# A Fourier, MLP and routing kernel: routing units, weight conversion and the hand-over to the kept tokens moved

## The chip, the cores and the metric

The kernel runs on one core of a Trainium2 chip. The metric is the time on the device, in microseconds (us), of one execution. Of the kernel before there are three timed runs, with a median of 1934.6 us, and one profiled execution.

A core has five engines that run their own queues in order: TensorE (PE, matmuls and transposes), VectorE (DVE), ScalarE (ACT), GpSimd (POOL) and SyncE (SP, which here only issues DMAs). They meet through semaphores. PSUM is the memory that PE writes to, SBUF the one that all of them read.

## The reference

```python
def _attn_ref(x):                        # x: 8 x 3072 x 256
    X = np.fft.fft(x, axis=1)
    X = np.fft.fft(X, axis=2)
    return X.real.astype(np.float32)

def _moe_ref(x, w_in, w_out, alpha):     # 256 -> 2048 -> 256
    h = x @ w_in
    g = np.maximum(h, 0.0) + alpha * np.minimum(h, 0.0)
    return (g @ w_out).astype(np.float32)

def _moe2_ref(x, w_gate, w1, w2, capacity):   # 8 experts, capacity 768
    logits = x @ w_gate
    expert_idx = np.argmax(logits, axis=1)
    probs = softmax(logits)                   # written out in the reference
    gate_w = probs[np.arange(N), expert_idx]
    ...                  # tokens in order: the first 768 of each expert are kept
    h = np.maximum(np.einsum('ecd,edf->ecf', disp, w1), 0.0)
    y = np.einsum('ecf,efd->ecd', h, w2)
    ...                  # out[i] = gate_w[i] * y[expert, pos] if kept, else 0
```

The 8 batches are flattened to 24576 tokens before the MLP. Each expert keeps 768, so at most 6144 tokens need the MLP in full; the others need only their gate logits, and an output row of zeros.

## The kernel before

**Three stretches.** The first 59.5 us load constants and weights and do stage 1 of the Fourier transform of batch 0. Then come eight batches, to 1068 us, which compute gate logits of all tokens and route them. From 1091.9 us to the end 16 tiles of 384 kept tokens (8 experts, two tiles each) go through the MLP and their expert.

**A batch** has 32 steps, numbered (b, s), each a call of `fstep`: six matmuls q, a copy qs of q by ACT (L494), qm by DVE (L495), six matmuls p, and mp and mm by DVE (L505, L506). q has one PSUM buffer and p two. Every fourth step (s % 4 == 1; in batch 0 every step) a logit block follows: 4 calls of `logit`, 32 matmuls that reduce mp and mm to gate logits.

**What else runs in a step** stands in three lists filled by `at(list, b, t, fn, ...)`, where t counts steps from the start of batch b: `pre` runs ahead of `fstep`, `early` between qm and the p matmuls, `late` behind the logit block (L837 to 846). Since every engine's queue is in order, this sets what stands behind what. In these lists are, for the batches to come: the load of x (SP), its fold (xf, POOL or DVE), fsplit (fh on ACT, fl on POOL), stage 1 (matmuls into an mi buffer of PSUM, then the copy zw on ACT, L255), stage 2 (s), transp, and split.

**In batch 0** the weights are converted as well. `conv_a` and `conv_b` take a chunk i of w_in (k = "i") or w_out (k = "o") apart: an ACT Square into a tile m (L366), then DVE; `conv_c` finishes on POOL. m has two buffers, which wf of `w_cs` shares (L395). `w_cs`, `w_t`, `w_b` and `w_h` turn chunks into the tables of the logits, on PE, ACT and DVE. Chunk i is used at steps around s = 4 i.

**The route units of a batch** run inside the next one. `ltrans` turns logits (ls) by three transposes and copies them back (lst, ACT). u0: maximum and dd on DVE, exp on ACT (L575). u1: one-hot of the expert (DVE). u2: matmuls that count tokens ahead of each in its expert, into mi, the copy pc (ACT, L595), the addition of the counts so far (carry), and the sum of the exps. u3: the slot number idx of each token (DVE). Then 24 scatters (`us`): POOL copies one column of the latest mm to `gate` (L627), which ties the scatter to that step, and issues an indirect DMA of 128 records (L628).

**The hand-over** (L847 on): `ltrans` and the route units of the last batch without steps around them, then `rows`, which finds the table rows of the first 9 x 128 slots by a product of one-hot matrices (hotp, from DVE; hotr, from DVE and POOL) instead of reading back a scatter. Then POOL gathers three times 128 rows (L942), DVE turns signs (L953), PE transposes, and the first tile starts. In a tile, step f of `hstep` makes h (PE), ng (ACT, L978), g (DVE, L979), gh (ACT, L980) and gl (POOL, in the first tile DVE, L981); `ystep` uses gh and gl three steps later. W1 and W2 of the first expert are split in two parts by `split_w` (ACT copy and DVE subtraction, L934 and L935). `heat` issues matmuls whose result is not used.

## Time and profile before

| | |
|---|---|
| timed runs, median of 3 | 1934.6 us (1932.71 to 1936.72) |
| the profiled execution's own time | 1926.48 us |
| its span | 1924.7 us |
| mean granted clock of TensorE, share of full speed | 0.986 |
| PE busy | 1865.5 us, 97% |
| DVE busy | 1191.6 us, 62% |
| ACT busy | 851.0 us, 44% |
| POOL busy | 1109.7 us, 58% |

All rows are of the profiled execution; its start is 0. PE is busy for nearly all of the span, so the other engines matter where PE waits for them. A row of an instruction names its engine, line, operation and what it writes and reads (out<-in), with buffer numbers left out. What stands in brackets at its end is how long the engine had been idle, and what it waited for last.

### The profile page before, as it was taken

What the parts mean: (1) busy time and instruction counts of PE and PEld (TensorE: products, weight loads), DVE (VectorE), ACT (ScalarE), POOL (GpSimd) and SP (SyncE); (2) the same over time, 40 slices, a digit from 0 to 9 for tenths busy, and PEclk for the clock granted to TensorE, in tenths of its full rate; (3) what the DMA queues carried; (4) which work ended last, traced back from release to release, by engine and by line L of the source; (5) the groups of instructions that cost most, each with busy time, mean ns of one, the idle gap of its engine ahead of it and who ended that gap; (6) DMA issues with size and microseconds to landing.
All of it is one profiled execution on the core that took longest, in us unless ns stands there. A gap on an engine that the chain in (4) does not pass through costs nothing. (4 is left out here: it accounts for less than half of the span.)

```text
span 1924.7 us, 33959 instructions
## 1 busy us (share of the span) xinstructions
PE 1865.5 (97%) x12965; PEld 1604.0 (83%) x12965; DVE 1191.6 (62%) x1684; ACT 851.0 (44%) x1712; POOL 1109.7 (58%) x1230
## 2 busy tenths in 40 slices
PE   8899999999999999999999899999999999999997
PEld 5676687777777777777777699999999999999997
DVE  4799588878989989898899653333333333333331
ACT  3445455444344343443322254545444444444452
POOL 3675394867767676674435375645455555555452
PEclk9799999999999999999999999999999999999999
DMA  9644345444353443433310301101111111101000
GB/s 262 203 147 133 103 156 189 128 131 149 105 165 118 142 153 109 161 116 113 101 34 1 141 16 62 34 33 36 37 39 39 39 36 39 40 15 61 15 9 17
DMA packets 126259, 174.48 MB, mean 91 GB/s; under 512 B 20060, under 2 KB 80285, under 8 KB 125488
## 3 DMA queue, kind: packets, MB, share of 16 engines
q1 hardware_dynamic: 115056, 157.99, 25.8%
q0 software_dynamic: 10752, 12.23, 2.3%
q8 instruction: 102, 1.67, 0.4%
q10 hardware_dynamic: 288, 2.10, 0.3%
q14 instruction: 61, 0.50, 0.1%
HBM read 94.71 MB, written 78.40 MB: 90 GB/s over the span
## 5 line engine op out<-in xcount | busy, mean ns | idle before, releaser
L981 POOL TENSOR_TENSOR gl<-g,gh 128x384 fp32r<-128x384 f32 x240 | 243.4, 1014 | 324.1 <-ACT gh L980 323.1
L495 DVE SCALAR_TENSOR_TENSOR qm<-er,w,qs 128x780 f32<-128x780 f32 x256 | 322.6, 1260 | 119.1 <-ACT qs L494 115.8
L494 ACT COPY qs<-q 128x780 f32<-128x780 f32 x256 | 207.6, 811 | 335.7 <-PE q L491 159.3
L979 DVE SCALAR_TENSOR_TENSOR g<-ng,om,h 128x384 f32<-128x384 f32 x256 | 157.1, 614 | 313.8 <-ACT ng L978 272.4
L993 PE MATMUL y<-gh,WO 128*128 128x384 f32 x1024 | 262.2, 337 | 0.0
L505 DVE SCALAR_TENSOR_TENSOR mp<-p,qs 128x780 f32<-128x780 f32 x256 | 245.7, 960 | 5.2 <-PE p L501 5.2
L506 DVE TENSOR_TENSOR mm<-p,qm 128x780 f32<-128x780 f32 x256 | 244.8, 956 | 0.0
L628 POOL DMA_INDIRECT rec<-recs,idx x192 | 197.3, 1028 | 56.0 <-issue 45.7
L980 ACT CAST gh<-g 128x384 fp32r<-128x384 f32 x256 | 131.6, 514 | 197.9 <-DVE g L979 197.9
L978 ACT ACTIVATE ng<-h 128x384 f32<-128x384 f32 x256 | 125.8, 491 | 176.4 <-PE h L972 176.2
L518 PE MATMUL lg<-mp,Vn 128*32 128x384 f32 x1024 | 187.7, 493 | 0.2 <-DVE mp L505 0.2
L993 PEld LDWEIGHTS y<-gh,WO 128*128 128x128 f32 x1024 | 186.8, 188 | 0.0
L518 PE MATMUL lg<-mm,Vp 128*32 128x384 f32 x1024 | 184.3, 493 | 0.1
L993 PE MATMUL y<-gl,WO 128*128 128x384 f32 x512 | 172.7, 337 | 0.0
L1015 DVE SCALAR_TENSOR_TENSOR z<-z,z 128x384 fp32r<-128x384 f32 x128 | 71.3, 557 | 162.2 <-ACT z L1014 162.2
L627 POOL COPY gate<-mm 128x1 f32<-128x1 f32 x168 | 79.0, 470 | 137.9 <-DVE mm L506 137.8
L1025 PE MATMUL o<-W,z 128*128 128x256 f32 x1152 | 154.7, 284 | 1.2 <-ACT ot L1028 1.2
L1025 PEld LDWEIGHTS o<-W,z 128*128 128x128 f32 x1152 | 146.9, 190 | 1.6 <-ACT ot L1028 1.6
L238 POOL TENSOR_TENSOR fl<-xf,fh 128x512 fp32r<-128x512 f32 x72 | 96.5, 1341 | 79.3 <-ACT fh L237 68.2
L1012 PE MATMUL z<-yh,W 128*128 128x384 f32 x512 | 130.5, 335 | 0.4
L518 PEld LDWEIGHTS lg<-mp,Vn 128*32 128x32 f32 x1024 | 55.6, 110 | 88.2 <-issue 84.2
L501 PE MATMUL p<-Ah,w20r 128*128 128x390 f32 x256 | 92.3, 361 | 5.2 <-DVE mm L506 5.1
(353 smaller groups left out, 4537.6 us busy)
## 6 DMA issues: line engine op xcount, KB each, us to landing
x<-x SPq DMA_DIRECT2D x96, 256.0 KB, 3.4
zd<-zw SPq DMA_DIRECT2D x96, 256.0 KB, 2.1
out_dram<-zero SPq DMA_DIRECT2D x64, 384.0 KB, 4.6
zk<-zd SPq DMA_DIRECT2D x240, 96.0 KB, 2.8
r<-w SPq DMA_DIRECT2D x16, 1024.0 KB, 5.6
abtab<-tm SPq DMA_DIRECT2D x60, 256.0 KB, 2.4
er<-erd SPq DMA_DIRECT2D x16, 390.0 KB, 4.4
rawi<-w_in SPq DMA_DIRECT2D x8, 512.0 KB, 4.4
```

Source lines behind the costliest of these rows:

```text
L494: A.copy(qs, q[:, :, 0:SB])
L495: V.scalar_tensor_tensor(out=qm, in0=e, scalar=w2[:, f : f + 1], in1=qs, op0=ALU.mult, op1=ALU.add)
L505: V.scalar_tensor_tensor(out=mp, in0=p[:, :, 0:SB], scalar=-1.0, in1=qs, op0=ALU.mult, op1=ALU.min)
L506: V.tensor_tensor(out=mm, in0=p[:, :, 0:SB], in1=qm, op=ALU.max)
L518: PE.matmul(l[32 * gi : 32 * gi + 32, 0:384], lhsT=w, rhs=v, start=start, stop=stop)
L628: d = G.indirect_dma_start(out=rec, out_offset=bass.IndirectOffsetOnAxis(ap=st["idx"][:, i : i + 1], axis=0), in_=recs[:, b].rearrange("p ...
L979: V.scalar_tensor_tensor(out=g, in0=ng, scalar=om[:, f : f + 1], in1=ps, op0=ALU.mult, op1=ALU.add)
L980: A.copy(gh, g)
L981: (V if i == 0 else G).tensor_tensor(out=gl, in0=g, in1=gh.bitcast(F32), op=ALU.subtract)
L993: PE.matmul(d["yp"][m][:, 0:384], lhsT=w[:, f, ms], rhs=x, start=(f == 0 and n == 0), stop=(f == NF - 1 and n == 2))
L1012: PE.matmul(ps, lhsT=w[:, kd, ms], rhs=x, start=(n == 0), stop=(n == 5))
L1025: PE.matmul(ps, lhsT=x[:, m, js], rhs=w[:, m, :], start=(m == 0 and n == 0), stop=(m == 7 and n == 2))
```

## The change

Five edits, in the words of what they do:

1. The conversion of chunk 3 of w_in and w_out (`conv_a`, `conv_b`, `conv_c`, and the load of the next chunk) runs one step later in batch 0. The loads of x of the second batch, from its third block, run one step later.
2. All route units run in `late`, and u2 is cut in two: u2 keeps the matmuls and the copy pc, u2b has the addition of the counts, the update of carry and the sum of the exps (`norm`).
3. The steps of these units and of the scatters change: for the units of the second to sixth batch the scatters stand at steps 18 to 41, so that the last ten run in the batch after. The last ones stand at steps 10 to 30, three steps having two.
4. In the hand-over the last batch reads PSUM without the copies lst and pc, leaves carry as it is, and runs `norm` behind the gathers. Of the one-hot matrix hotp DVE makes 16 of 24 columns, and ACT the others as Relu(1 - (iota - p)^2), from a new tile npj = -p. The product takes four columns of DVE and two of ACT in turn.
5. The W1 split of the first expert moves from ahead of the signs into steps f = 8 to 11 of the first tile. The transposes of the first tile run gather by gather, with 5 heat matmuls between.

The names in the excerpts below carry the batch and the step or chunk: mi3 is m of chunk 3 of w_in, zw1_2 is zw of batch 1, block 2, qs3_0_5 is qs of batch 3, half 0, step 5. Several rows of an instruction with the same operands are one row with a count.

ACT in batch 0, steps 1 and 2, first before and then after:

```order
L366 ACTIVATE mo2_904<-rawo2_783 128x512
L366 ACTIVATE mi3_916<-rawi3_849 128x512
L255 COPY zw1_2_924<-mi_921 128x512
L494 COPY qs0_1_1_943<-q0_1_1_936 128x780
L437 COPY uu1_954<-mi_947 64x256
L441 COPY wgs_116<-mi_947 128x2x8
```

```order
L367 ACTIVATE mo2_903<-rawo2_782 128x512
L256 COPY zw1_2_917<-mi_914 128x512
L495 COPY qs0_1_1_936<-q0_1_1_929 128x780
L438 COPY uu1_947<-mi_940 64x256
L442 COPY wgs_117<-mi_940 128x2x8
L397 COPY wf2_963<-mi_958 128x512
L400 CAST w10r_954<-wf2_963 128x256
L400 CAST w12r_956<-wf2_963 128x256
L402 ACTIVATE wr2_967<-wf2_963 1x2x128
L367 ACTIVATE mi3_988<-rawi3_848 128x512
L256 COPY zw1_3_996<-mi_993 128x512
```

The Square mi3 stood ahead of zw1_2; it now stands nine rows later, directly ahead of zw1_3.

ACT in batch 3, steps 2 to 6, where the route units of batch 2 run (lst2, ex2, pc2), first before and then after:

```order
L494 COPY qs3_0_2_5800<-q3_0_2_5793 128x780
L237 CAST fh4_10_5815<-xf4_10_5728 128x512
L553 COPY lst2_5824<-mi_5820 128x384
L477 CAST Bh3_1_5836<-Bf3_4729 128x780
L494 COPY qs3_0_3_5853<-q3_0_3_5846 128x780
L575 ACTIVATE ex2_5861<-dd2_5859 128x192
L494 COPY qs3_0_4_5881<-q3_0_4_5874 128x780
L255 COPY zw4_10_5892<-mi_5885 128x512
```

```order
L495 COPY qs3_0_4_5841<-q3_0_4_5834 128x780
L256 COPY zw4_10_5852<-mi_5845 128x512
L238 CAST fh4_11_5866<-xf4_11_5798 128x512
L555 COPY lst2_5875<-mi_5871 128x384
L478 CAST Ah3_1_5885<-Af3_4671 128x780
L495 COPY qs3_0_5_5907<-q3_0_5_5900 128x780
L578 ACTIVATE ex2_5943<-dd2_5941 128x192
L495 COPY qs3_0_6_5964<-q3_0_6_5957 128x780
```

The exp stood between the qs copies of steps 3 and 4; it now stands between those of steps 5 and 6.

DVE in the hand-over, from the counts of the last batch to the row numbers, first before and then after:

```order
L598 TENSOR_TENSOR tp7_12662<-pc7_12660,carry_81 128x192
L599 TENSOR_TENSOR carry_81<-pc7_12660,carry_81 128x8
L602 TENSOR_REDUCE sm7_12665<-ex7_12635 128x24
L603 TENSOR_SCALAR sm7_12665<-sm7_12665 128x24
L604 RECIPROCAL recs_80<-sm7_12665 128x24
L608 TENSOR_TENSOR tp7_12662<-tp7_12662,oh_84 128x192
```

```order
L606 TENSOR_TENSOR tp7_12659<-mi_12642,carry_81 128x192
L620 TENSOR_TENSOR tp7_12659<-tp7_12659,oh_85 128x192
L622 TENSOR_REDUCE pos7_12662<-tp7_12659 128x24
L624 TENSOR_SCALAR ov7_12664<-pos7_12662 128x24
L625 SCALAR_TENSOR_TENSOR pos7_12662<-r7_12638,pos7_12662 128x24
```

The four rows between the two tp rows are gone from here; three of them (L614 to L616) now stand behind the row numbers, and the product with oh follows at once.

The diff, cut:

```diff
@@
+    npj = cp.tile([128, 24], F32, name="npj")
@@
             PE.transpose(ps[:, j, :], ls[:, 128 * j : 128 * j + 128], ident)
-        lt2 = sp.tile([128, 384], F32, name=f"lst{b}", tag="ls", bufs=1)
-        A.copy(lt2.rearrange("p (j r) -> p j r", j=3), ps)
-        v0 = lt2.rearrange("p (j g a e) -> p g a j e", j=3, g=4, e=8)
+        if b < NB - 1:
+            lt2 = sp.tile([128, 384], F32, name=f"lst{b}", tag="ls", bufs=1)
+            A.copy(lt2.rearrange("p (j r) -> p j r", j=3), ps)
+            ps = lt2.rearrange("p (j r) -> p j r", j=3)
+        v0 = ps.rearrange("p j (g a e) -> p g a j e", g=4, e=8)
         for pi in range(2):
@@
                 PE.matmul(ps[:, :, q + 1 :, :], lhsT=rk[:, 4, :], rhs=ohs[:, q : q + 1, :].unsqueeze(1).to_broadcast([128, 2, 12 - q, 8]), start=False, stop=(q == 11), skip_group_check=True)
-            pc = rt([128, 2, 13, 8], "pc")
-            A.copy(pc, ps)
-            ps = pc
+            if b < NB - 1:
+                pc = rt([128, 2, 13, 8], "pc")
+                A.copy(pc, ps)
+                ps = pc
+            st["ps"] = ps
+
+        def u2b():
+            ps = st["ps"]
             t = rt([128, 2, 12, 8], "tp")
             V.tensor_tensor(out=t, in0=ps[:, :, 0:12, :], in1=carry.unsqueeze(1).unsqueeze(1).to_broadcast([128, 2, 12, 8]), op=ALU.add)
-            V.tensor_tensor(out=carry, in0=ps[:, 0, 12, :], in1=carry, op=ALU.add)
             st["t"] = t
+            if b < NB - 1:
+                V.tensor_tensor(out=carry, in0=ps[:, 0, 12, :], in1=carry, op=ALU.add)
+                norm()
+
+        def norm():
             sm = rt([128, 24], "sm")
@@
                 V.tensor_copy(pjf, pj)
+                V.tensor_scalar(out=npj, in0=pj[:, 0], scalar1=-1.0, scalar2=None, op0=ALU.mult)
             V.scalar_tensor_tensor(out=idx, in0=pj[:, 0], scalar=float(NJ), in1=pj[:, 1], op0=ALU.mult, op1=ALU.add)
@@
-        return [u0, u1, u2, u3], [us(i) for i in range(24)]
+        return [u0, u1, u2, u2b, u3], [us(i) for i in range(24)], norm
@@
         if i > 1:
-            for k, t in (("i", s - 10), ("o", s - 8)) if i > 2 else (("i", 1), ("o", 2)):
+            for k, t in (("i", s - 10 + (i == 3)), ("o", s - 8 + (i == 3))) if i > 2 else (("i", 1), ("o", 2)):
                 at(late, 0, t, conv_a, k, i)
@@
                 if c > 1:
-                    at(pre, 0, c - 3, load_x, nb, c)
+                    at(pre, 0, c - 2, load_x, nb, c)
                     at(pre, 0, c - 1, fold, nb, c)
@@
         if nb < NB:
-            rl, r1 = ((13, 14, 15, 17, 18), 19) if nb == 1 else ((6, 7, 8, 9, 10), 11) if nb == 2 else ((2, 3, 4, 5, 6), 7)
+            if nb == 1:
+                rl, r1 = (14, 15, 17, 19, 21, 23), range(24, 48)
+            elif nb < NB - 1:
+                rl, r1 = (4, 5, 9, 11, 13, 17), range(18, 42)
+            else:
+                rl, r1 = (2, 3, 5, 6, 7, 9), sorted([*range(10, 31), 13, 17, 21])
             at(late, nb, rl[0], ltrans, b)
-            ru, rs = route_units(b)
-            for i in range(4):
-                at(late if i == 2 else early, nb, rl[i + 1], ru[i])
+            ru, rs, _ = route_units(b)
+            for i in range(5):
+                at(late, nb, rl[i + 1], ru[i])
             for i in range(24):
-                at(pre, nb, r1 + i, rs[i])
+                at(pre, nb, r1[i], rs[i])
 
@@
     ltrans(NB - 1)
-    ru, scat = route_units(NB - 1)
+    ru, scat, norm = route_units(NB - 1)
     HT = (13, 45, 30)
@@
 
+    one = kp.tile([128, 1], F32, name="one")
+    G.memset(one, 1.0)
+
     def rows():
@@
             G.tensor_tensor(out=R[:, w], in0=H, in1=rk[:, 6, 24 * w : 24 * w + 24].unsqueeze(2).to_broadcast([128, 24, NJ0]), op=ALU.mult)
-        for c in range(0, 24, 6):
-            hot(V, P, 0, c, c + 6)
-        for c in range(24):
+        for c in range(0, 16, 4):
+            hot(V, P, 0, c, c + 4)
+        for c in range(16, 24):
+            sq = k2.tile([128, 128], F32, name=f"sq{c}", tag="ng")
+            A.activation(out=sq, in_=iota, func=AF.Square, bias=npj[:, c : c + 1])
+            A.activation(out=P[:, c], in_=sq, func=AF.Relu, scale=-1.0, bias=one)
+        order = [4 * (k // 6) + k % 6 if k % 6 < 4 else 16 + 2 * (k // 6) + k % 6 - 4 for k in range(24)]
+        for c in order:
             PE.matmul(ps, lhsT=P[:, c], rhs=R[:, :, c], start=(c == 0), stop=(c == 23))
@@
             PE.transpose(ps[:, 128 * j : 128 * j + 128], d["gr"][:, j, 128 * w : 128 * w + 128], ident)
+        prep_x(i, w, ps)
+
+    def prep_x(i, w, ps):
+        d = tiles[i]
         h = k2.tile([128, 384], F32R, name=f"xh{i}_{w}", tag=f"xh{w}")
@@
         prep_gather(0, j)
-    for o in range(4):
-        split_w(1, o, V)
+    norm()
+    tr = [ps1.tile([128, 512], F32, name=f"tp0_{w}", tag=t) for w, t in ((0, "tp"), (1, "o"))]
+    hz = ps2.tile([128, 512], F32, name="heat", tag="z")
     for j in range(3):
         prep_sign(0, j)
-    prep_tr(0, 0)
-    prep_tr(0, 1, "o")
+        for w in range(2):
+            PE.transpose(tr[w][:, 128 * j : 128 * j + 128], tiles[0]["gr"][:, j, 128 * w : 128 * w + 128], ident)
+        if j < 2:
+            heat(hz, 5)
+    for w in range(2):
+        prep_x(0, w, tr[w])
     load_wo(A, 1)
@@
                 scat[16 * i + f]()
-            if i == 0 and f >= 12:
-                split_w(2, f - 12, V)
+            if i == 0 and f >= 8:
+                split_w(1 + f // 12, f % 4, V)
             if (i, f) == (1, 9):
```

## Rows read from the trace of the kernel before

**Rows 1.** Page, its head: the span and the number of instructions.

```profile
span 1924.7 us, 33959 instructions
```

**Rows 2.** PE's waits by releaser: us in all, number, longest in us.

```profile
PE p L501 <- DVE mm L506: 5.3, 10, 1.0
...
PE mi L431 <- ACT zw L255: 5.1, 1, 5.1
PE mi L250 <- POOL fl L238: 4.9, 4, 1.9
PE q L491 <- ACT qs L494: 4.8, 6, 1.2
```

**Rows 3.** Windows: length; PE, PEld, DVE, ACT, POOL busy (x); clock; DMA; GB/s.

```profile
82.50:92.70 10.20, 9.11 (x34) 6.67 (x34) 6.89 (x10) 3.23 (x8) 6.87 (x10) 0.50 0.58 182
...
413.60:417.00 3.40, 3.40 (x25) 2.49 (x24) 2.46 (x3) 1.19 (x3) 2.84 (x3) 0.52 0.26 88
...
1092.90:1096.30 3.40, 3.40 (x13) 3.40 (x12) 1.18 (x3) 1.34 (x3) 0.00 (x0) 0.52 0.89 352
```

**Rows 4.** Timeline of ACT, batch 0: start, length, instruction.

```profile
81.82 0.67 ACT L366 ACTIVATE mi<-rawi 128x512 f32<-128x512 f32 x1 [4.40 <-DMA rawi<-w_in]
82.39 0.57 ACT L255 COPY zw<-mi 128x512 f32<-128x512 f32 x1
...
94.28 0.59 ACT L255 COPY zw<-mi 128x512 f32<-128x512 f32 x1 [2.32 <-PE mi L250]
```

**Rows 5.** Timeline of POOL and DVE, batch 0.

```profile
85.89 1.59 POOL L384 TENSOR_TENSOR wo<-fro,mo 128x512 f32<-128x512 f32 x1
...
91.36 0.42 DVE L404 TENSOR_TENSOR w11r<-wf,w10r 128x256 fp32r<-128x256 f32 x1 [3.05 <-ACT w10r L399]
```

**Rows 6.** Timeline of PE, batches 2 and 3.

```profile
413.47 1.11 PE L305 MATMUL s<-zk,GT 48*32 48x256 f32 x16 [1.41 <-issue]
...
490.27 0.39 PE L250 MATMUL mi<-fl,fr 128*128 128x258 f32 x1 [0.95 <-POOL fl L238]
```

**Rows 7.** Page, costliest groups: busy, mean ns, idle before.

```profile
L505 DVE SCALAR_TENSOR_TENSOR mp<-p,qs 128x780 f32<-128x780 f32 x256 | 245.7, 960 | 5.2 <-PE p L501 5.2
```

**Rows 8.** Timeline of ACT, hand-over.

```profile
1069.43 0.48 ACT L553 COPY lst<-mi 128x384 f32<-128x384 f32 x1 [0.69 <-PE mi L551]
...
1073.71 0.33 ACT L595 COPY pc<-mi 128x208 f32<-128x208 f32 x1 [1.83 <-PE mi L593]
```

**Rows 9.** Timeline of DVE, hand-over.

```profile
1074.47 0.17 DVE L599 TENSOR_TENSOR carry<-pc,carry 128x8 f32<-128x8 f32 x1
...
1075.37 0.29 DVE L608 TENSOR_TENSOR tp<-tp,oh 128x192 f32<-128x192 f32 x1
...
1077.92 4.26 DVE L898 TENSOR_TENSOR hotp<-rk,pjf 128x768 bf16<-128x768 bf16 x4
...
1083.56 2.50 DVE L935 TENSOR_TENSOR W<-r,W 128x512 fp32r<-128x512 f32 x4
```

**Rows 10.** Timeline of POOL, hand-over.

```profile
1083.65 1.57 POOL L942 DMA_INDIRECT gr<-abtab,ixr  x1 [3.15 <-DVE sg L886]
...
1087.24 1.00 POOL L942 DMA_INDIRECT gr<-abtab,ixr  x1 [0.31 <-issue]
```

**Rows 11.** Timeline of ACT, batch 0, a chain of copies.

```profile
90.31 0.58 ACT L396 COPY wf<-mi 128x512 f32<-128x512 f32 x1 [3.94 <-POOL Vp L442]
90.92 0.40 ACT L399 CAST w10r<-wf 128x256 fp32r<-128x256 f32 x1
91.23 0.40 ACT L399 CAST w12r<-wf 128x256 fp32r<-128x256 f32 x1
```

**Rows 12.** Timeline of DVE, first tile.

```profile
1115.86 0.61 DVE L979 SCALAR_TENSOR_TENSOR g<-ng,om,h 128x384 f32<-128x384 f32 x1
...
1117.96 0.61 DVE L979 SCALAR_TENSOR_TENSOR g<-ng,om,h 128x384 f32<-128x384 f32 x1
...
1120.48 0.61 DVE L979 SCALAR_TENSOR_TENSOR g<-ng,om,h 128x384 f32<-128x384 f32 x1
```

## The prediction, made before the changed kernel had run

> **What bounds the kernel now.** I read the page's head first: the span of the profiled execution is 1924.7 us [rows 1], its own time 1926.48 us, and the three timed runs have a median of 1934.6 us. The difference of 8 us lies between executions, so I add up changes against the profiled execution and carry the sum over to the median. PE is the engine that the table of the profile shows as busy almost throughout, so the end moves only where PE waits, or where it runs at the lower of its two clock levels. Hence the second view, PE's waits by releaser [rows 2]. Four of its lines touch the change: p matmuls that wait for DVE's mm (5.3 us in 10 waits), the small gate product on mi that waits for ACT's zw copy (one wait of 5.1), stage 1 that waits for POOL's fl (4.9 in 4), and q matmuls that wait for ACT's qs (4.8 in 6). Third, the stretches with a low granted clock [rows 3]: 82.5 to 92.7 at 0.50, 413.6 to 417.0 at 0.52, and 1092.9 to 1096.3 at 0.52, where 1.0 is 2.4 GHz. In each of them PE comes out of a wait. A stall here costs its own length and then about as much again at half speed. Last I read the timeline of each place where these waits lie, and of the hand-over from the last batch to the first tile of kept tokens.
>
> **Batch 0: the Square of chunk 3 of w_in.** Before, ACT's queue has that Square at 81.82 us; it waits 4.40 for its DMA, and zw of stage-1 block 2 stands behind it at 82.39 although its input is long there [rows 4]. PE's 5.1 us wait is that. The first order excerpt shows the Square moved behind four later copies. What is late next: the Square shares the m buffer with the product wo on POOL, which ends at 85.89 + 1.59 = 87.48 [rows 5], so Square and the next zw (chunk 3) come at about 88.1, against 94.28 now [rows 4], which is 6.2 earlier. DVE has little slack behind that: the largest idle time of this stretch is the 3.05 us before w11r at 91.36 [rows 5], a wait for ACT, not for work. So the gain can fade; bounds 0 and -6.2, and I take **-5.5**, near the upper end, because the wait is PE's own and the half-clock stretch begins with it. The load of x a step later makes two DMAs later, with a fold three steps ahead of use; SP has nothing else waiting there. I price it at nothing (up to 1 us if a fold becomes late).
>
> **Route units behind the logit blocks, batches 1 to 7.** The units are the same DVE, ACT and PE instructions; they move. Before, u0, u1 and u3 stand between qm and the p matmuls, so mm of the step comes late and PE waits for it: 5.3 us [rows 2]. Behind a logit block PE has its 32 matmuls in hand. I leave 0.8 us for the places where the spacing is narrow: **-4.5** (bounds 0 and -5.3). In batch 2 the same backlog shows as a wait of 1.41 before the s matmuls [rows 6] and then 3.4 us at 0.52 [rows 3], which is 3.4 x 0.48 = 1.6 lost: **-3.0**.
>
> The exp on ACT waits for DVE's dd, and qs stands behind it. The second order excerpt shows ex2 before between qs of steps 3 and 4, now behind qs of step 5, which follows a logit block. The largest q wait is 1.2, in batch 7; the other five make 4.8 - 1.2 = 3.6, of which I take **-3.4**. In batch 7 u0 is late in step 3, which has no logit block; dd now stands behind mp and mm, each 0.96 us [rows 7], so the exp delays qs by up to 1.9 more: **+1.9** (bounds 0 and +1.9).
>
> Two new costs. The scatters now run from step 18 to 41 of 32, that is across the border of two batches, where POOL has xf and fl of the next-but-one x. A wait of stage 1 for fl there was 0.95 in batch 3 [rows 6]; I take three such, for batches 4 to 6: **+2.9** (bounds 0 and what the slow rival gives). u2 takes an mi buffer in a step where transp also uses one, so its matmuls wait for one ACT copy; the nearest row is 0.31 from start to start of two 128x256 casts [rows 11], in six batches: **+1.9** (bounds 0 and 4).
>
> **The hand-over.** Off the chain from the last logit block to the gathers go the lst copy (0.48, with its hand-over 0.54), the pc copy (0.33) and, between 1074.47 and 1075.37, carry and norm: 0.90 [rows 8, 9]. npj adds 0.10. Together -1.7. The one-hot P of 4.26 us [rows 9] is cut: DVE makes 16 of 24 columns, 4.26 x 16/24 = 2.84, and would begin at 1077.92 - 1.7 = 1076.2 and end at 1079.1. ACT makes the other 8 by a Square and a Relu each. No such pair stands in the trace. The nearest rows are two casts 128x256 [rows 11]: a dependent instruction starts 0.03 after the end of the one before (wf 90.31 + 0.58, w10r 90.92), an independent one 0.09 before it. For half the elements I estimate 0.29, a pair 0.29 + 0.03 + 0.29 - 0.09 = 0.52, eight 4.2 us; begun with npj, about 0.4 ahead of DVE's P, that ends at 1080.0, against 1082.18 for the old P. Bounds of a pair 0.34 (half of the pair of casts, overlapped) and 0.76 (two casts of the larger size): ends 1078.5 and 1081.9. So the end of the rows product moves by **-2.2** (bounds -3.1 and -0.3).
>
> The Trainium skill, "ScalarE: Activation LUTs", section Rules for kernel authors, budgets about 0.3 us per ACTIVATE with a bias read from a column, plus 0.83 ns an element. By it 16 of them are 16 x 0.41 = 6.5 us, ACT would end at about 1082.3, the gain of 2.2 would be gone and the time 2.2 longer; the trace has 0.40 for a cast of 256 elements without such a bias, where the rule makes 0.51, and no row with one. That lies inside the forecast's own range below.
>
> The gathers: with the W1 split beside them on DVE (1083.56, 2.50 long) the first took 1.57 us, the third without it 1.00 [rows 9, 10]. Without the split I take **-1.0** for the three (bounds 0 and -1.0). The Trainium skill, "SBUF - State Buffer", section Who interferes with whom, speaks against this: a tensor_tensor takes only the read side of the pair that DVE and GpSimd share, and descriptor generation needs the write side (it calls that inferred). By it the split never slowed the gathers and this term is 0, so the time is 1.0 longer; the rows lean the other way, but the first gather may be long as the first.
>
> The first h matmuls run at 0.52 for 3.4 us [rows 3], 1.6 lost. Now transposes and heat matmuls stand between the gathers, so I take half: **-0.8**. The W1 split goes into the first tile at f = 8 to 11. There DVE's g comes every 2.10 us without W (1115.86 to 1117.96) and 2.52 with W and a sign [rows 12]; two steps with a sign make 2 x 0.42, the two others I put at half that: **+1.3** (bounds 0 and 1.7), since PE waits for gl of each step.
>
> **Sum.** -5.5 - 4.5 - 3.0 - 3.4 + 1.9 + 2.9 + 1.9 - 2.2 - 1.0 - 0.8 + 1.3 = -12.4. On the profiled execution 1914.1, on the median 1934.6 - 12.4 = 1922.
>
> **Rivals.**
> More is gained: the prologue keeps all 6.2, the clock stays up at the first tile (0.8 more), and the three new costs (1.9, 2.9, 1.9) lie under PE work. That is 8.2 more, 1914. For it: in the batches the long waits of PE are few, so a late fl may meet a PE with work in hand; against: a queue that runs in order hands every delay on.
> The gain of batch 0 is given back: the conversions of w_in and w_out are a chain over ACT, DVE and POOL, and PE waits later for the next chunk. Then 5.5 is lost and the time is 1927.5. For it: the DVE idle before 91.36 is a wait for ACT, so everything there is late at once.
> No change: the exp still stalls qs, only at another step, because dd is last on DVE behind mp and mm of the step in all batches. Then the 3.4 stays and four batches pay 1.9: -12.4 + 3.4 + 7.6 = -1.4, 1933. Against: the logit block before it gives ACT the time of 32 matmuls on PE. This is also the case in which the change doesn't do what it says.
> Slower: POOL falls behind at the batch borders. A gate copy waits for the latest mm in POOL's queue, with the scatter, fold and fl behind it; if this makes fl late for five stage-1 blocks in each of the batches 4 to 6 by the longest wait in the list, 1.9 [rows 2], that is 15 x 1.9 = 28.5 instead of 2.9: -12.4 + 25.6 = +13, 1948. It decides the sign from nine such waits on (9 x 1.9 = 17 instead of 2.9). Against: the scatters lay on other steps of the same queue before, with four waits in all.
>
> **How the numbers follow.** Forecast 0.55 (own range 1916 to 1928), more 0.13, given back 0.15, no change 0.09, slower 0.08. A measurement of this kernel can tell about 0.2% (3.9 us): faster is below 1930.7, slower above 1938.5. Faster: 0.53 of the forecast, 0.13, and 0.12 of the third case, 0.78. Same: 0.09 and the rest of these, with part of the open ends, 0.13. Slower: 0.09. The range 1911 to 1934 leaves out the slow case and the edges, about 0.14.
>
> **What would show it.** In the profile after: no PE wait of 5 us for zw near 82 us, and clock 1.0 from there; the line p for mm under 1 us; the q wait for qs about 0.2 plus one of 3 in batch 7; fl waits at the borders of batches 4 to 6 near 1 us each; the last P column at 1080 on the old time axis, three gathers at 1.0 each; g every 2.5 us at f = 10 and 11. The forecast is wrong if batch 0 ends less than 3 us earlier, if the fl waits pass 10 us, or if ACT's pairs take 0.7 us.

## The result and the profile after

| | before | changed |
|---|---|---|
| timed runs, median of 4 | 1933.65 us (1931.89 to 1936.72) | 1913.67 us (1912.07 to 1914.42) |
| profiled execution: own time, span | 1926.48, 1924.7 us | 1913.86, 1911.8 us |
| mean granted clock | 0.986 | 0.989 |

The ratio is 0.9894, with a 95% interval of 0.9877 to 0.9911: 17 to 24 us less. Forecast were 12.4 less on the profiled execution and 1922 on the median. Between the two profiled executions it is 12.6 less in time and 12.9 in span; on the medians it is 20.0, 8.3 below the forecast. So there are two questions: did the terms come out as worked out, and where do the other 7 us on the medians come from?

PE's waits in the profile after (us in all, times, longest), the lines that answer to [rows 2] and what is new:

```profile
PE mi L251 <- POOL fl L239: 8.0, 7, 2.2
PE mi L251 <- POOL xf L231: 7.5, 3, 5.2
...
PE q L492 <- ACT qs L495: 3.5, 3, 3.0
PE mi L251 <- ACT wf L397: 3.0, 1, 3.0
PE rows L932 <- ACT hotp L929: 2.5, 5, 0.5
PE tp L985 <- DVE xl L993: 2.4, 1, 2.4
...
PE p L502 <- DVE mm L507: 1.5, 3, 0.9
```

The 5.1 us for zw are gone (a wait of 1.4 for a later zw, at another line, has come), and the waits for mm fell from 5.3 to 1.5. The q waits are three now, and one makes nearly all of them. Longer are fl (three waits more), xf, and xl, which was 0.5 before; new are wf, and hotp from ACT (hotp from DVE was 0.9 before).

Batch 0, in the order of [rows 4]: ACT's Square of chunk 3 and the zw behind it, then wf near 113 and what PE waits for there.

```profile
89.14 0.68 ACT L367 ACTIVATE mi<-rawi 128x512 f32<-128x512 f32 x1 [2.40 <-POOL wo L385]
89.72 0.58 ACT L256 COPY zw<-mi 128x512 f32<-128x512 f32 x1
```

```profile
112.87 0.58 ACT L397 COPY wf<-mi 128x512 f32<-128x512 f32 x1 [5.08 <-POOL wo L385]
```

```profile
113.51 0.93 PE L251 MATMUL mi<-xf,f 128*128 128x258 f32 x2 [3.01 <-ACT wf L397]
```

The Square now waits for POOL's product wo, since they share the buffer m, and zw comes at 89.72 instead of 94.28. But wf shares m as well: the next wf waits 5.08 us for the next wo, and PE 3.01 behind it. By windows over the whole batch (length, busy times of five engines with counts, the clock; before, then after) PE's idle time did not fall: 11.7 us, then 12.7. What fell is the time lost to the lower clock: 8.0 us, then 5.1, summed over the granted clock of the batch.

```profile
59.47:238.28 178.81, 167.11 (x1130) 118.39 (x1130) 147.29 (x181) 80.93 (x171) 103.35 (x109) 0.96 0.45 143
```

```profile
59.66:236.62 176.96, 164.22 (x1130) 117.99 (x1129) 152.91 (x181) 81.04 (x171) 103.17 (x109) 0.97 0.46 144
```

Batches: the border of 2 and 3 (the same 0.94 stands at the borders 3/4, 4/5 and 5/6), and the exp of the last batch with PE behind it.

```profile
483.50 0.39 PE L251 MATMUL mi<-fl,fr 128*128 128x258 f32 x1 [0.94 <-POOL fl L239]
```

```profile
966.28 0.36 ACT L578 ACTIVATE ex<-dd 128x192 f32<-128x192 f32 x1 [4.37 <-DVE dd L576]
```

```profile
967.40 0.69 PE L492 MATMUL q<-Bh,w12r 128*128 128x390 f32 x1 [3.04 <-ACT qs L495]
```

And the clock there, as in [rows 3] (length, busy times of five engines with counts, then the clock):

```profile
964.40:971.20 6.80, 3.80 (x16) 3.55 (x18) 5.15 (x8) 2.62 (x4) 3.48 (x6) 0.75 0.01 1
```

Behind the wait of 3.04 PE is at the lower level for a while: this window of 6.8 us has a mean clock of 0.75, which loses 1.7 more. (In the profile with x loaded early, below, the same wait has no such stretch behind it, and the batch is 1.4 shorter; a stall does not always cost as much again at half speed.)

The hand-over: ACT's first pairs, DVE's first row behind the product (before, then after), POOL's second gather before and its three after, and PE's wait in the first tile.

```profile
1067.14 0.40 ACT L928 ACTIVATE sq<-rk,npj 128x128 f32<-128x128 bf16 x1 [4.92 <-DVE hotr L919]
1067.62 0.40 ACT L929 ACTIVATE hotp<-sq,one 128x128 bf16<-128x128 f32 x1
1067.93 0.39 ACT L928 ACTIVATE sq<-rk,npj 128x128 f32<-128x128 bf16 x1
...
1072.70 0.40 ACT L929 ACTIVATE hotp<-sq,one 128x128 bf16<-128x128 f32 x1
```

```profile
1082.59 0.17 DVE L908 TENSOR_TENSOR vf<-rows,recp 128x9 f32<-128x9 f32 x1 [0.41 <-PE rows L906]
```

```profile
1073.39 0.17 DVE L934 TENSOR_TENSOR vf<-rows,recp 128x9 f32<-128x9 f32 x1 [3.14 <-PE rows L932]
```

```profile
1085.53 1.41 POOL L942 DMA_INDIRECT gr<-abtab,ixr  x1 [0.30 <-issue]
```

```profile
1074.46 1.08 POOL L968 DMA_INDIRECT gr<-abtab,ixr  x1 [5.35 <-DVE sg L904]
1075.84 1.01 POOL L968 DMA_INDIRECT gr<-abtab,ixr  x1 [0.30 <-issue]
1077.15 1.00 POOL L968 DMA_INDIRECT gr<-abtab,ixr  x1 [0.30 <-issue]
```

```profile
1115.55 0.55 PE L985 MATMUL tp<-con,gr 128*128 128x128 f32 x3 [2.39 <-DVE xl L993]
```

A column on ACT takes 0.72 us (a Square of 0.39 to 0.40 and a Relu of 0.40, overlapping little), so eight end at 1073.10, far behind DVE's sixteen at 1070.25. DVE's vf starts 14.27 us after the last copy ls (1059.12), and 14.34 before (1068.25): no gain at all. The gathers are 1.0 each, without the W split beside them.

Last, a tile in the middle: the ng copies of its first step and of the next tile's, first before, then after.

```profile
1433.95 0.49 ACT L978 ACTIVATE ng<-h 128x384 f32<-128x384 f32 x1 [0.63 <-PE h L972]
...
1485.08 0.49 ACT L978 ACTIVATE ng<-h 128x384 f32<-128x384 f32 x1 [0.63 <-PE h L972]
```

```profile
1424.06 0.49 ACT L1008 ACTIVATE ng<-h 128x384 f32<-128x384 f32 x1 [0.62 <-PE h L1002]
...
1474.86 0.49 ACT L1008 ACTIVATE ng<-h 128x384 f32<-128x384 f32 x1 [0.62 <-PE h L1002]
```

Both kernels in a window of 51 us of this stretch, with the counts of recorded matmuls and the clock:

```profile
1600.00:1651.00 51.00, 51.00 (x319) 50.93 (x319) 16.36 (x30) 25.87 (x54) 29.29 (x28) 1.00 0.11 37
```

```profile
1600.00:1651.00 51.00, 51.00 (x321) 50.93 (x320) 16.84 (x31) 26.43 (x56) 32.46 (x31) 1.00 0.18 58
```

51.13 us before, 50.80 after, with the same instructions of PE, PE never idle and the clock at 1.00. Over 14 tiles this is 4.7 us that no term of the prediction had.

By stretches, from the profiles of the two and of the experiments below (us; a batch from its first qs copy to the next one's, the hand-over from the copy ls to the first h matmul, then the first two tiles, one later tile, and the span):

| kernel | batch 0 | 1 | 2 | 3 | 4 to 6 | 7 | hand-over | 2 tiles | tile | span |
|---|---|---|---|---|---|---|---|---|---|---|
| before | 178.8 | 122.0 | 126.6 | 121.7 | 355.0 | 104.7 | 23.7 | 86.4 | 51.13 | 1924.7 |
| before, again | 178.0 | 122.1 | 127.1 | 122.5 | 356.5 | 104.8 | 23.6 | 88.1 | 51.13 | 1929.4 |
| changed | 177.0 | 121.3 | 122.1 | 119.1 | 351.6 | 108.4 | 22.6 | 88.4 | 50.79 | 1911.8 |
| changed, again | 177.3 | 121.3 | 123.7 | 119.0 | 351.5 | 108.2 | 22.8 | 87.2 | 50.79 | 1912.0 |
| only edit 1 | 174.9 | 122.1 | 128.2 | 122.5 | 356.2 | 104.6 | 23.7 | 89.4 | 51.13 | 1928.1 |
| only the route units | 178.5 | 121.5 | 121.2 | 118.9 | 351.9 | 108.5 | 23.7 | 86.6 | 51.13 | 1916.8 |
| only the hand-over | 175.7 | 121.9 | 129.4 | 122.5 | 356.2 | 104.8 | 22.3 | 87.2 | 50.80 | 1921.7 |
| before, 96 bytes inserted | 178.2 | 121.9 | 126.5 | 121.6 | 354.9 | 104.7 | 23.7 | 86.2 | 50.87 | 1920.1 |
| x loaded early | 173.2 | 121.3 | 123.6 | 119.0 | 352.1 | 107.0 | 22.6 | 86.7 | 50.79 | 1906.4 |
| u0 at a logit step | 173.1 | 121.3 | 123.7 | 119.0 | 351.6 | 104.8 | 22.6 | 88.7 | 50.79 | 1906.6 |
| 20 columns on DVE | 176.3 | 121.3 | 122.1 | 119.0 | 352.2 | 109.7 | 20.4 | 86.7 | 50.79 | 1910.9 |
| streamed operands moved | 173.6 | 121.3 | 122.6 | 118.8 | 351.8 | 108.5 | 22.6 | 88.0 | 50.77 | 1908.0 |
| splits later | 174.4 | 121.3 | 122.6 | 118.8 | 351.7 | 108.5 | 22.5 | 85.2 | 50.79 | 1905.8 |
| all three improvements | 175.0 | 121.3 | 122.2 | 119.0 | 351.7 | 104.8 | 20.5 | 90.3 | 50.80 | 1906.8 |

Each row is one execution. The two of the kernel before differ by 1.7 in the first two tiles and by 1.5 in batches 4 to 6, the two of the changed kernel by 1.6 in batch 2, so a difference of 2 us in one stretch of one profile says little.

### The profile page after: what moved, and what is told of

The parts are those of the page before. It is cut to its first block, busy times and chain, and to the rows that moved or that the text cites. A ratio compares the mean times of both kernels' runs of the same rounds, so it can differ in the third digit from the quotient of the medians.

```text
span 1911.8 us, 34003 instructions
## 1 busy us (share of the span) xinstructions
PE 1854.9 (97%) x12975; PEld 1599.0 (84%) x12975; DVE 1189.1 (62%) x1684; ACT 856.1 (45%) x1726; POOL 1102.6 (58%) x1231
## 5 line engine op out<-in xcount | busy, mean ns | idle before, releaser
L496 DVE SCALAR_TENSOR_TENSOR qm<-er,w,qs 128x780 f32<-128x780 f32 x256 | 329.2, 1286 | 121.0 <-ACT qs L495 114.2
L1008 ACT ACTIVATE ng<-h 128x384 f32<-128x384 f32 x256 | 125.6, 490 | 173.1 <-PE h L1002 171.3
L640 POOL COPY gate<-mm 128x1 f32<-128x1 f32 x168 | 71.4, 425 | 110.8 <-DVE mm L507 110.7
L229 POOL TENSOR_TENSOR xf<-x 128x254 f32<-128x254 f32 x84 | 95.6, 1138 | 9.5 <-DMA x<-x 8.5
```

What stands on the lines that cost most here:

```text
L496: V.scalar_tensor_tensor(out=qm, in0=e, scalar=w2[:, f : f + 1], in1=qs, op0=ALU.mult, op1=ALU.add)
```

## The experiments

Three sets, each on one chip beside runs of the kernel before; medians of those were 1932.8, 1925.3 and 1933.7 us.

**The kernel before, again** (first set; no edit).

> The kernel before, unchanged, profiled once more. In the two profiles in hand a tile of kept tokens takes 51.13 us before and 50.79 after, 0.66% less, though its instructions are the same. Theory 1, the rate of PE differs from one execution to the next: here the tile comes out elsewhere than 51.13, and the time moves with it; the ratio is 1.000. Theory 2, the tile is slower because of something in the kernel before (where its buffers lie): it is 51.13 again, within 0.05. In either case the waits of PE that the change touches are there again: zw 5.1 near 78 us, mm 5.3, fl 4.9, qs 4.8.

1932.9 us, ratio 1.0009 (1.0000 to 1.0018). The tile is 51.13 again, so the difference lies in the kernel, not in the execution; that it is the place of the buffers is for a run below. The waits differ in size: zw 3.3 instead of 5.1. Batches 2 to 6 and the first two tiles were 4.5 us longer than in the first profile: that one was a short execution. And the wait for xl in the first tile is 1.9 here, 0.5 in the first profile, with no edit between them:

```profile
PE tp L959 <- DVE xl L963: 1.9, 1, 1.9
```

**x loaded early** (first set).

```diff
-                    at(pre, 0, c - 2, load_x, nb, c)
+                    at(pre, 0, c - 3, load_x, nb, c)
```

> The changed kernel with the loads of x of the second batch one step earlier again, as before. Theory 1, the later load is what made the wait for xf near 62 us 5.16 instead of 2.73, with half speed behind it: that wait is 2.7 again, PE gains 2.4 at once and batch 0 is 2.4 to 4 us shorter (time about 1910 to 1911 where the changed kernel has 1913.7). Theory 2, the fold waits for POOL's and ACT's conversion work and not for the load: the wait stays near 5 and the time is the same within 1 us.

1911.2 us, ratio 0.9896 (0.9879 to 0.9912), the same as the changed kernel. The wait for xf was 3.5 here, 3.3 and 2.7 in two other profiles with the late load, and 5.0 in the kernel with only the route units, which has the early one. So it varies from one execution to the next, and the edit is worth nothing that can be told: neither the 5.16 nor its disappearance is shown to be the load's doing.

**u0 of the last batch at a logit step** (first set).

```diff
-                rl, r1 = (2, 3, 5, 6, 7, 9), sorted([*range(10, 31), 13, 17, 21])
+                rl, r1 = (2, 5, 5, 6, 7, 9), sorted([*range(10, 31), 13, 17, 21])
```

> The changed kernel with u0 and u1 of the units in the last batch in step 5, which has a logit block, instead of steps 3 and 5. Theory 1, the q wait of 3.04 us near 964 comes from the exp, whose input stands behind mp and mm of step 3 on DVE: the wait goes, and the half speed behind it (0.73 and 0.77 over 6.8 us), together 3.0 to 4.7 us less, batch 7 near 104 us instead of 108.4. Theory 2, any place of the exp stalls qs here, since DVE has two mp and two mm to do per step: a wait of 2 us or more shows at step 6, and the time is the same within 1 us.

1909.6 us, ratio 0.9881 (0.9865 to 0.9896), beside 0.9894 for the changed kernel. Batch 7 took 104.8 instead of 108.4, the 3.04 is gone, and no stretch of the batch is at the lower clock. PE's waits for qs in all:

```profile
PE q L492 <- ACT qs L495: 0.5, 2, 0.3
```

Theory 1.

**20 columns of P on DVE, 4 on ACT** (first set).

```diff
-        for c in range(0, 16, 4):
-            hot(V, P, 0, c, c + 4)
-        for c in range(16, 24):
+        for c in range(0, 20, 5):
+            hot(V, P, 0, c, c + 5)
+        for c in range(20, 24):
```

(The order of the product follows: five columns of DVE, one of ACT.)

> The changed kernel with 20 columns of the one-hot matrix P on DVE and 4 on ACT instead of 16 and 8. ACT's column took 0.72 us there (two instructions of 0.40 that overlap by 0.09 at one end), DVE's 0.20. Theory 1, ACT's half sets the end of the rows product (1073.36 in the changed kernel): ACT now ends after 2.9 us, DVE after 3.9, the rows product ends 1.9 to 2.2 us earlier after the last logit block, and the time falls by as much. Theory 2, the rows product waits for POOL's hotr or the following steps wait for another thing: the end moves by less than 0.7 us.

From ls to the first h matmul 20.4 us instead of 22.6. DVE's 20 columns and the row behind the product:

```profile
1070.08 3.74 DVE L919 TENSOR_TENSOR hotp<-rk,pjf 128x640 bf16<-128x640 bf16 x4
1074.22 0.17 DVE L934 TENSOR_TENSOR vf<-rows,recp 128x9 f32<-128x9 f32 x1 [0.40 <-PE rows L932]
```

Theory 1 for the stretch, 2.1 less. In the time it does not show: 1913.2 us, 0.9899 (0.9883 to 0.9914). Batch 7 and the prologue were each longer by 1.3 and 1.9 us in the profiled execution; an effect of 2 us is within what runs differ by.

**96 bytes inserted into the kernel before** (second set).

```diff
     pjf = cp.tile([128, 2, 24], BF16, name="pjf")
+    pad = cp.tile([128, 24], F32, name="pad")
```

> The kernel before with one more tile of 96 bytes a partition declared behind pjf, never written or read, no other change: no instruction is added. In the kernel before the expert weights W1 and W2 and the table WO start 32 bytes past a multiple of 64 in each partition; npj, which the change adds at this place, moves them to a multiple of 64. A tile of kept tokens took 51.13 us in both profiles of before and 50.79 in all four profiles of the changed kernel and its variants. Theory 1, the place of the weights sets this: the tile is 50.79 here, 14 to 15 tiles make 4.8 to 5.1 us, ratio about 0.9975. Theory 2, it comes from the edits of the hand-over (another state of the engines when the tiles begin): the tile is 51.13, ratio 1.000.

1921.3 us beside 1925.3, ratio 0.9977 (0.9968 to 0.9986): 2.7 to 6.2 us from moving tiles, with no instruction changed. The tile:

```profile
1431.69 0.49 ACT L979 ACTIVATE ng<-h 128x384 f32<-128x384 f32 x1 [0.63 <-PE h L973]
...
1482.55 0.49 ACT L979 ACTIVATE ng<-h 128x384 f32<-128x384 f32 x1 [0.63 <-PE h L973]
```

50.86 us: the place of the tiles makes most of the 0.34, and 0.07 are left over. But all tiles behind the new one moved, and theory 1 names the weights. The traces tell more. By windows over this tile with one line each (length, PE's busy time, the time of its weight loads, the clock), the matmuls of y, whose weights are WO, before and with the 96 bytes, then those of z, whose weights are W1:

```profile
1433.95:1485.08 51.13, 19.26 (x98) 17.09 (x97) 1.00 0.12 37
1431.69:1482.55 50.86, 19.05 (x98) 16.86 (x97) 1.00 0.12 37
```

```profile
1433.95:1485.08 51.13, 9.64 (x48) 8.44 (x48) 1.00 0.12 37
1431.69:1482.55 50.86, 9.60 (x48) 8.43 (x48) 1.00 0.12 37
```

Over twelve tiles a matmul of y starts 175.9 ns after the matmul ahead of it before, and 173.3 here and in the changed kernel; with 96 of them in a tile that is 0.25 us. Between matmuls of z it is 173.4 and 173.3, though W1 moved by the same 96 bytes from the same remainder. So it is the place of WO that pays, and the remainder by 64 alone does not decide it. Most of the 0.07 stands in o: 121.4 ns between its matmuls before and here, 120.6 in the changed kernel.

**The streamed operands moved too** (second set).

```diff
-    one = kp.tile([128, 1], F32, name="one")
+    one = kp.tile([128, 16], F32, name="one")[:, 0:1]
```

> The changed kernel with the tile of the constant one 64 bytes long instead of 4, so that the operands which PE streams (xh, gh, gl, yh, z) start at a multiple of 64 bytes as well; in the changed kernel they are 32 bytes past one. Theory 1, only the weights' place matters: the tile stays at 50.79 within 0.03, the time the same. Theory 2, the place of streamed operands costs as well: the tile falls further, to 50.5 or less, 4 us or more in all.

1913.3 us, and a tile of 50.77: no effect beyond 0.02. Theory 1 for xh, gh, gl and yh. z does not belong in that list: in the o matmuls it is the stationary operand, and W2 is streamed. There 120.1 ns lie between two matmuls instead of 120.6, which makes the 0.02 to 0.03.

**Only the route units** (second set; edits 2 and 3 put into the kernel before, and nothing else).

```diff
-            rl, r1 = ((13, 14, 15, 17, 18), 19) if nb == 1 else ((6, 7, 8, 9, 10), 11) if nb == 2 else ((2, 3, 4, 5, 6), 7)
+            if nb == 1:
+                rl, r1 = (14, 15, 17, 19, 21, 23), range(24, 48)
+            ...
```

> The kernel before with only the route units moved (u2 cut in two, all units behind the logit blocks, scatters at their new steps); weight conversion, hand-over, W1 split and the place of all tiles as before. Theory 1, what batches 1 to 7 gained comes from this edit alone: they take 121.3, 122.1, 119.0, 119.3, 119.0, 113.3 and 108.4 us as in the changed kernel (7.5 less in all than before), batch 0 stays near 178.4 and the hand-over at 23.7, time about 1926. Theory 2, part of it is the place of the tiles, which the changed kernel moved: batches 3 to 6 lie at least 0.7 us above those numbers.

1919.3 us beside 1925.3, ratio 0.9968 (0.9956 to 0.9980). The table shows batches 1 to 7 as in the changed kernel, all else as before: theory 1.

**The splits of W1 and W2 later** (second set).

```diff
-            if i == 0 and f >= 8:
-                split_w(1 + f // 12, f % 4, V)
+            if i == 0 and f >= 12:
+                split_w(1, f - 12, V)
...
-            if pv > 0 and TT[pv][1] == 0 and 2 <= f < 6:
-                split_w(2, f - 2)
+            if pv >= 0 and TT[pv][1] == 0 and 2 <= f < 6:
+                split_w(2, f - 2, G if pv else V)
```

> The changed kernel with the W1 split of the first expert at f = 12 to 15 of the first tile (where the W2 split stood), and the W2 split at f = 2 to 5 of the second tile, on DVE. Theory 1, the two splits in eight steps in a row are what makes PE wait 2.39 us for xl at 1113 and lengthens the first tile by 2.9 (33.61 to 36.52): the wait falls to 0.5 or less and the first two tiles are 1.5 to 3 us shorter. Theory 2, DVE's backlog only moves to the second tile, whose z steps wait for W2 or whose xl comes late: the two tiles together stay within 0.7.

1910.0 us, ratio 0.9921 (0.9908 to 0.9934), beside 1913.3, ratio 0.9935 (0.9922 to 0.9948), of the streamed-operand kernel above in the same set: the intervals overlap. The first two tiles took 85.2 us instead of 88.4, and the wait for xl is short again:

```profile
1109.47 0.55 PE L985 MATMUL tp<-con,gr 128*128 128x128 f32 x3 [0.51 <-DVE xl L993]
```

For the wait this is theory 1, with a limit. In some executions ACT stands for 1.0 to 1.8 us ahead of step 10 or 11 of the first tile: in the changed kernel's first profile, but also in the second one of the kernel before, where W1 is split ahead of the tile. Without that stand the wait for xl is 0.5 in three profiles without a split in these steps and 0.5 here, and 1.6 to 1.9 in five with the split at f = 8 to 11. So the split there costs 1.1 to 1.4 at this wait, and the rest of the 2.39 is ACT's stand. Of the 3.2 us between 85.2 and 88.4 some belongs to that and to a stretch at the lower clock at the first h matmuls, which this profile does not have; two profiles with the early split and with neither took 86.7, so about 1.5 is the split's, as far as three profiles tell.

**The changed kernel, again** (third set).

> The changed kernel once more, beside the runs of the kernel before on this chip. The kernel before had a median of 1932.8 us in one set of runs and 1925.3 in another, while the changed kernel and its variants stayed near 1913 in both. Theory 1, the size of the gain depends on the chip, since the kernel before moves with it: here the difference is between 11 and 20 us and agrees with the level of before (12 if before is near 1925, 20 if near 1933). Theory 2, the gain is 20 us on any chip, and the low level of before was that set's alone: the ratio is 0.9894 again within 0.0015 whatever the level of before.

1912.9 us, ratio 0.9891 (0.9876 to 0.9905), with before at 1933.7. In this set the rule of theory 1 (20 us where before is near 1933) and theory 2 say the same, so it decides nothing by itself. The second set speaks for theory 1: there a kernel that differs from the changed one by the length of one tile had 1913.3 beside a before of 1925.3, 12 us less.

**Only edit 1** (third set).

```diff
-            for k, t in (("i", s - 10), ("o", s - 8)) if i > 2 else (("i", 1), ("o", 2)):
+            for k, t in (("i", s - 10 + (i == 3)), ("o", s - 8 + (i == 3))) if i > 2 else (("i", 1), ("o", 2)):
...
-                    at(pre, 0, c - 3, load_x, nb, c)
+                    at(pre, 0, c - 2, load_x, nb, c)
```

> The kernel before with only the conversion of chunk 3 and the loads of x of the second batch one step later. Batch 0 took 178.0 to 178.8 us in four profiles without this edit and 173.2 to 177.0 in six with it, other edits beside. Theory 1, the edit alone does this: batch 0 between 173 and 177, the wait for zw near 80 us is gone, a wait of 2 to 3 us for wf stands near 110 in its place, all later stretches are as before; 2 to 5 us less, ratio 0.9975 to 0.9990. Theory 2, batch 0 profits from another edit: 178 or more, ratio 1.000.

1929.7 us, ratio 0.9977 (0.9967 to 0.9986). In batch 0 the 5 us for zw are gone, and the waits in their place are there without any other edit:

```profile
PE mi L250 <- ACT wf L396: 3.0, 1, 3.0
PE mi L419 <- ACT zw L255: 2.1, 1, 2.1
```

Theory 1. Batch 0 itself is a weak witness: 174.9 here, but 175.7 in the next kernel, which does not have the edit.

**Only the hand-over** (third set; the changed kernel with edits 1 to 3 undone, of which the steps of the units are shown; u2b runs behind u2).

```diff
-            if nb == 1:
-                rl, r1 = (14, 15, 17, 19, 21, 23), range(24, 48)
...
+            rl, r1 = ((13, 14, 15, 17, 17, 18), 19) if nb == 1 else ((6, 7, 8, 9, 9, 10), 11) if nb == 2 else ((2, 3, 4, 5, 5, 6), 7)
...
-                at(late, nb, rl[i + 1], ru[i])
+                at(late if i in (2, 3) else early, nb, rl[i + 1], ru[i])
```

> The kernel before with only the changed hand-over (no copies lst and pc in the last batch, norm behind the gathers, one-hot matrix shared between DVE and ACT, W1 split in the first tile, transposes gather by gather, the new tiles npj and one). Theory 1: from the last logit block to the first h matmul 22.5 us instead of 23.7, the first two tiles 0 to 2 us longer, and each later tile 50.8 instead of 51.13 because npj moves the weights: 4 to 5 us less in all, nearly all of it from the place of the weights, ratio 0.9970 to 0.9985. Theory 2, the shorter chain itself is what pays: first tiles no longer than before and 6 us or more less.

1924.4 us, ratio 0.9957 (0.9944 to 0.9969): 6 to 11 us, more than theory 1's ratio. The profile gives theory 1's pieces: hand-over 22.3, first two tiles no shorter than they vary, and 50.80 for each later tile, 4.6 in all. Beside the second profile of before, 2.3 more lie in batch 0, which no part of this edit touches. So about 6 us are shown as its own, 4.6 of them by the place of the tiles.

**All three improvements** (third set; the edits of the last batch, of P and of the splits together).

> The changed kernel with the three improvements that single runs showed: u0 and u1 of the last batch in step 5 (3.6 us less in batch 7), 20 of 24 one-hot columns on DVE (2.1 less in the hand-over), W1 split at f = 12 to 15 of the first tile and W2 split in the second tile (1.5 to 3 less in the first two tiles). Theory 1, they lie in different stretches and add: 7 to 9 us below the changed kernel on the same chip, near 1905. Theory 2, they overlap (the clock or the first tile's DVE takes part back): 5 us or less.

1908.2 us, ratio 0.9871 (0.9857 to 0.9885): 4.7 less than the changed kernel beside it, not 7 to 9. The number is theory 2's. Batch 7 and the hand-over gave their 3.4 and 2.3, but the first two tiles took 90.3 us. In the profiled execution ACT stood 1.73 us in step 9 of the first tile, and the wait for xl was back:

```profile
PE tp L985 <- DVE xl L993: 1.9, 1, 1.9
```

What held ACT there is open, and the edits need not be its cause: it stood 1.71 us at the same step in the second profile of the kernel before, 1.36 in the changed kernel's first and not in its second. The kernel has the lowest median of the case; its four runs (1907.5 to 1909.5) all lie below the four of the changed kernel beside it, while its interval overlaps those of two of its parts.

## Why the prediction came out as it did

The time, 1913.7, is inside the range of 1911 to 1934, but below the forecast's own 1916 to 1928. It stands at the 1914 of the rival that gains more, by none of that rival's reasons: in these profiles batch 0 did not keep 6.2, the clock at the first tile did not stay up, and the new costs showed as waits of PE. On the first pair of profiles the sum is nearly exact, -12.4 against -12.9. That is luck: the terms are not exact, and their errors cancel. Two of the prediction's three signs of being wrong came: batch 0 ended 1.7 us earlier, not 3, and ACT's pairs took 0.72. The third, fl waits past 10 us, did not (8.0).

| term | forecast | first profiles | second profiles |
|---|---|---|---|
| batch 0 | -5.5 | -1.9 | -0.7 |
| batches 1 to 7 | -4.2 | -7.5 | -9.3 |
| ls to the first h matmul | -3.2 | -1.1 | -0.8 |
| first two tiles (clock, W1 split) | +0.5 | +2.0 | -0.9 |
| 14 later tiles | 0 | -4.7 | -4.7 |
| span, with the prologue | -12.4 | -12.9 | -17.4 |

**Batch 0.** The wait named went, and the Square waits for wo as forecast, with zw 4.6 us earlier. (It moved behind eight rows of ACT, five of them copies; the nine rows and the four copies above are miscounts, on which nothing rests.) What failed is the choice near the upper end of the bounds: the rival that gives the gain back was in part right, by the m buffer, which wf shares and which I followed for one chunk only. What is left of the gain is time at the lower clock, not idle time. Five profiles without edit 1 have a mean of 177.8 us in batch 0, nine with it 175.0 (one of them with the early load of x); on timed runs the edit alone gave 4.0 (2.7 to 6.4).

**Batches.** Step by step these held. The waits for mm fell by 3.8 (forecast 4.5). Batch 2 lost its 1.41 and the half speed behind it. The exp went behind a logit block in batches 3 to 6, and these waits went, 3.1 of 3.4. In the last batch the wait is 3.04, where 1.2 and 1.9 had been worked out; the 1.7 of the clock behind it was not. The three fl waits at the borders are 0.94 each, as worked out. u2's waits for mi make 1.1 (forecast 1.9). The waits add to about -2.6, and by windows PE's idle time over the seven batches went from 19.3 to 16.4, so no wait of size is missing. The other 4.6 us of the 7.5 lie in PE's busy time. Of these 1.7 are the clock: batch 2 had two stretches at half speed before, each 1.7 lost, and the prediction saw only the one at 413.6.

```profile
379.30:382.70 3.40, 3.40 (x18) 2.42 (x20) 1.26 (x2) 1.21 (x2) 3.22 (x6) 0.51 0.20 77
```

After, batch 2 has none and the last batch has one. The stretch near 413 is in all five profiles without edits 2 and 3 and in none of the nine with them. The one near 379 is not their doing: the second profile of the kernel before lacks it, and the second of the changed kernel has it. The last 2.9 us I can't lay to single rows. PE's ends of matmuls are modelled, and small stalls may hide in them: batch 3, before and after, by windows.

```profile
486.85:608.50 121.65, 118.22 (x932) 90.88 (x933) 107.06 (x124) 54.03 (x108) 89.20 (x109) 1.00 0.43 136
```

```profile
480.07:599.12 119.05, 117.54 (x932) 90.79 (x933) 104.33 (x124) 54.16 (x108) 82.22 (x101) 1.00 0.45 139
```

The same 932 rows take 0.7 us less at the same clock. The place of the tiles has no part in it, since the kernel with only the route units has the same batches.

**Hand-over.** The copies, carry and norm gave the 1.7: DVE's P starts 7.93 us after ls instead of 9.67. P then gave it all back. The step that failed is the price of a pair on ACT, 0.52 by two casts; it is 0.72. The Trainium skill, "ScalarE: Activation LUTs", section Rules for kernel authors, had it right: by it the estimate is 0.41 for such an ACTIVATE, measured 0.39 to 0.40, and a gain of nothing, as its sentence in the prediction said (the last column came at 1073.10, which is 1082.2 on the old axis, and the sentence has 1082.3). I had set it aside for rows of instructions without a bias from a column. The gathers gave 0.9 of 1.0, at the same two places in the queue: with a W split beside them 1.57 and 1.41, without 1.08 and 1.01. All five profiles with the split there and all nine without have these two times within 0.03. What the Trainium skill, "SBUF - State Buffer", section Who interferes with whom, infers of a tensor_tensor beside descriptor generation, no cost, these rows don't bear out. (The same section has a DVE instruction with two inputs in SBUF contend with a GpSimd instruction that reads SBUF; whether that is what slows a gather, no run here shows.)

**First tiles.** The +2.0 of the first profiles is not the edit's: the second pair has -0.9, and in the profiles without edit 5 the two tiles take 86.2 to 89.4. The W1 split cost 1.1 to 1.4 at the wait for xl, where 1.3 was put; the rest of the change from 0.5 to 2.39 there is ACT's stand, which the kernel before has too. For the clock half of 1.6 was put. The stretch at half speed at the first h matmuls is in all five profiles without edit 5 and in five of the nine with it, so the heat matmuls do not always keep the clock up, and both profiles of the changed kernel are among those that gained nothing.

**What was missing** is the place of the tiles. npj adds 96 bytes ahead of WO, W1 and W2, and PE goes through the same matmuls 0.66% faster. No term of the prediction had this; it makes 4.7 of the 20 us.

**And the base.** The sum made on one profile was carried to the median as it was; that profile was a short execution of the kernel before (1926.5, where the timed runs beside it have 1932 to 1937). On timed runs edit 1 alone gave 4.0 us, edits 2 and 3 gave 6.0, and edits 4 and 5 with their new tiles 9.3: 19.3 together, over two sets, which is the size of the whole. Part of that is clock: in the third set the runs of the kernel before had a mean granted clock of 0.984 and those of the changed kernel 0.989, and 0.45% of 1930 us is about 9 us, an estimate that takes PE as busy whenever the clock was low. Before moves between 1925 and 1934 from one set of runs to the next, while the changed kernel was at 1913.7 in the first result and 1912.9 in the third set, and its variant with the longer tile at 1913.3 in the second. Why, no run here settles.

## What to carry to other kernels

Follow a buffer that several operations share through all of its users: a wait taken from the first comes back at the third. Price an operation that the trace does not have by the rule that speaks of that very form, and only then by the nearest rows. When a change adds a tile, look at where the tiles behind it start, before a gain is put down to the edit that one meant. And take a second profile of the same kernel before a difference of 2 us in one stretch is called a term: what the kernel does by itself from one execution to the next was as large here.

## What the runs showed of the hardware that was not expected

Where a tile starts in SBUF can set how fast matmuls follow each other, and not for all of them. In the kernel before, WO, W1 and W2 start 32 bytes past a multiple of 64 in each partition. With 96 bytes ahead of them they start at a multiple of 64, and a tile takes 50.87 us instead of 51.13, and 50.77 to 50.80 in the changed kernel and its variants, at a clock of 1.00. Nearly all of it is in the matmuls with WO as stationary operand, 173.3 ns from the start of one to the next instead of 175.9; those with W1, which moved alike, had 173.4 and have 173.3. Why WO and not W1, no run here tells. The start of gh and gl, which these matmuls stream, does not matter: 173.3 with both 32 bytes past (the changed kernel) and with both at a multiple.

An indirect gather on POOL took 1.4 to 1.6 us beside a DVE subtraction with two inputs from SBUF (five profiles), and 1.0 to 1.1 without (nine).

Executions of one kernel differ in where PE's clock falls to the lower level: the stretch near 377 in batch 2 is in one of two profiles of the kernel before and in one of two of the changed kernel.
